# Inverse softmax sums by one small product and a way over DRAM, and K loaded for four heads at once, in a banded attention and mixture-of-experts kernel

## Chip, cores and metric

The kernel runs on one core of a Trainium2 chip. The metric is the device time of one execution in microseconds (us); the time of a kernel is the median of its runs.

## What is computed

Banded attention is followed by a mixture of experts. Attention has 4 batches, 8 heads, 768 positions and a head size of 64; each query sees the first 8 keys and the 96 keys up to itself, with a bias that grows with the distance.

```python
scores = scale * np.matmul(q, k.transpose(0, 1, 3, 2))
scores = np.where(keep, scores + bias, -1000000000.0)
a = np.exp(scores - scores.max(-1, keepdims=True))
a = a / (np.sum(a, axis=-1, keepdims=True) + 1e-09)     # the sums of the title
x = np.matmul(a, v)            # rearranged to 3072 x 512
# P: softmax of x @ w_gate, then 8 Sinkhorn iterations over rows and columns
for e in range(8):
    out += P[:, e:e + 1] * (np.maximum(x @ w1[e], 0.0) @ w2[e])
```

## The kernel before

**Units of work.** `Banded.work` lists 32 pieces n = (batch, half of the sequence, pair of heads g). A piece covers three query tiles of 128 (UT = 3) of two heads. `unit(u)` treats the four pieces of one batch and half; there are eight units. A piece has three groups of score tiles, so a unit has twelve groups t, taken two at a time (CHUNK) in six steps. With two pieces per six groups, a couple of pieces n = 2m and n = 2m + 1 spans three steps: t = 6m, 6m + 2 and 6m + 4.

**One step.** `ahead` computes scores and softmax four groups ahead (AHEAD). `flush` multiplies the turned scores of the step before with V into `o_ps`, and when a piece is complete it multiplies `o_ps` by `inv` on VectorE (line 404), casts it to `x` on ScalarE (line 405) and subtracts on VectorE (line 406). Then `turn` transposes the scores of this step (`t_ps`) and ScalarE copies them to `pT`. Then `between` is called three times: it emits filler work, which is the gate and the first layers of the mixture of experts for the unit before, and the sums `op` on GpSimd with their transfers to DRAM (`op_m`, from the pool `xout`). At the end of a step `prepare(n + 3)` transposes Q and K of a later piece and splits them into high and low parts (`qh`, `ql`, `kh`, `kl`), or, in the middle step of three, `invert` is called for both pieces. The filler lags by one unit and six slots, so the first unit has none.

**The inverse sums.** Exp leaves the sums of six columns (three tiles, two heads) on 128 query partitions. Line 316 adds EPS, line 317 inverts, and line 319 has ScalarE spread each column over 64 columns, to `inv` of 128 x 384. `invert` transposes its three tiles on TensorE into `r_ps`, and VectorE copies them back (line 414), so that each head's 64 partitions hold the row of inverse sums.

**PSUM.** `turned`, used by `prepare` and `invert`, takes a tile of tag "tp" from `self.ps`, which has two banks and serves `t_ps` also. In the first unit it takes the filler's banks, tag "fl", two as well.

**Loads.** All transfers are issued by SyncE, in one order. `load_qk(n)` loads Q of two heads with two transfers and K of two heads with five or seven, into `early_raw` for even n and `raw_qk` for odd n. It is called by `prepare(n - 2)`, once the buffer is free. `load_v(n)` loads V for four heads, thus for n and n + 1.

**Order.** TensorE's instructions keep the order of the program. On the other engines and on SyncE's queue a planner orders the instructions by its own reckoning of times. After attention come the dense layers by Strassen's scheme, to the end of the span; the change does not touch them.

Of the kernel before, what the change touches and what calls it, by code (L numbers as in the profile page):

```python
# [8 lines left out]
F32 = mybir.dt.float32  # L9
# [6 lines left out]
DRAM = bass.MemoryType.DRAM  # L16

P = 128
# [5 lines left out]
UT = 3  # L24
# [8 lines left out]
CHUNK = 2  # L33
# [81 lines left out]
class Banded:  # L115
# [5 lines left out]

    SLOTS = 8 * len(GROUPS)
    QK, V = UT + 4, 5
    RAW = QK * P + V * 2 * P
    BIAS1 = 4 * P

    SCRATCH = RAW + 3 * P

    def __init__(self, tc, q, k, v, early, n_bias):

        self.tc, self.nc = tc, tc.nc
        self.q, self.k, self.v = q, k, v
        self.H, self.D = q.shape[1], q.shape[3]
        assert n_bias == self.H * self.BIAS1
        self.bias1, rest = early, early[:, n_bias:]
        self.early_raw = rest[:, 0:self.RAW]
        self.d1 = early[:, n_bias - self.BIAS1:n_bias]
        self.d0 = rest[:, self.RAW:self.RAW + P]  # L140
        self.warm = rest[:, self.RAW + P:].bitcast(mybir.dt.bfloat16)
        self.work = [(b, half, g) for b in range(q.shape[0]) for half in range(2) for g in range(self.H // 2)]
        self.pending = []
        self.sums, self.inv, self.outs = {}, {}, {}
        self.pe = InOrder(tc)
        self.qk, self.vs, self.ready, self.scored = {}, {}, {}, {}

    def open(self, ctx, ident, idle):

        tc = self.tc  # L150
        self.ident, self.idle = ident, idle
        self.raw = ctx.enter_context(tc.tile_pool(name="f_raw", bufs=1, side="right"))
        self.bias0 = self.raw.tile([P, self.H, P], F32, name="bias0")
        self.opd = ctx.enter_context(tc.tile_pool(name="f_opd", bufs=2, side="right"))
        self.wrk = ctx.enter_context(tc.tile_pool(name="f_wrk", bufs=AHEAD + CHUNK, side="right"))
        self.ps = ctx.enter_context(tc.tile_pool(name="f_ps", bufs=2, space=PSUM))

    def distances(self, ng, nl):

# [57 lines left out]
            slot -= shift if slot > 1 + half else 0  # L217
            self.nc.sync.dma_start(out=dst[p:p + w, slot].rearrange("p (j d) -> p j d", j=heads), in_=src[row:row + w, tile])

    def load_qk(self, n):  # L220
        if n >= len(self.work):
            return
        b, half, g = self.work[n]
        if n % 2 == 0:
            t = self.early_raw[:, 0:self.QK * P]
        else:
            t = self.raw.tile([P, self.QK * P], F32, name="raw_qk")
        t = t.rearrange("p (t c) -> p t c", c=P)
        q_r, k_r = t[:, 0:UT], t[:, UT:]
        for j in range(2):  # L230
            src = self.q[b, 2 * g + j].rearrange("(t p) d -> p t d", p=P)
            self.nc.sync.dma_start(out=q_r[:, :, j * self.D:(j + 1) * self.D], in_=src[:, half * UT:(half + 1) * UT])
        self.load_heads(k_r, self.k, n, 2, [x for x in PIECES[half] if x[0] != 2 + half], 1)
        self.qk[n] = q_r, k_r

    def load_v(self, n):

        if n >= len(self.work):
            return
        if n % 4 == 0:  # L240
            t = self.early_raw[:, self.QK * P:]
        else:
            t = self.raw.tile([P, self.V * 2 * P], F32, name="raw_v")
# [8 lines left out]
    def prepare(self, n):  # L252

        if n >= len(self.work):
            return
        nc = self.nc
        self.ready[n] = tuple(self.opd.tile([P, w], F32R, name=name)
                              for name, w in (("qh", UT * P), ("ql", UT * P), ("kh", 4 * P + P // 2), ("kl", 4 * P + P // 2)))
        q_r, k_r = self.qk[n]
        qh, ql, kh, kl = self.ready[n]  # L260
        for src, hi, lo, nb in ((q_r, qh, ql, UT), (k_r, kh, kl, UT + self.work[n][1])):
            tp = self.turned("tp")
            for t in range(nb):
                self.pe.transpose(out=tp[:, t], in_=src[:, t], identity=self.ident)
            tp = tp.rearrange("p t c -> p (t c)")[:, 0:nb * P]
            nc.scalar.copy(out=hi[:, 0:nb * P], in_=tp)
            nc.vector.tensor_tensor(out=lo[:, 0:nb * P], in0=tp, in1=hi[:, 0:nb * P], op=ALU.subtract)
        self.load_qk(n + 2)

    def scores(self, ts):  # L270

# [21 lines left out]
    def softmax(self, t, s_list):  # L293


        nc, D = self.nc, self.D
        n, group = divmod(t, len(GROUPS))
        _, half, g = self.work[n]
        p_sb = self.wrk.tile([P, 2, 2, P], F32, name="p_sb")
        mx = self.wrk.tile([P, 2], F32, name="mx", bufs=4)  # L300
        if group == 0:
            self.sums[n] = self.wrk.tile([P, UT, 2], F32, name="sm", bufs=4)
        sm = self.sums[n]
        views = []
        for u, (j, i) in enumerate(GROUPS[group]):
            h = 2 * g + j
            pv = p_sb[:, u, 0:len(KEYS[half][i])]
            views.append(pv)
            nc.vector.tensor_tensor_reduce(out=pv, in0=s_list[u], in1=self.bias(h, half, i), scale=-(D ** -0.5), scalar=3.0e38,
                                           op0=ALU.add, op1=ALU.min, accum_out=mx[:, u:u + 1])  # L310
        for u, pv in enumerate(views):
            j, i = GROUPS[group][u]
            nc.scalar.activation(out=pv, in_=pv, func=AF.Exp, bias=mx[:, u:u + 1], scale=-1.0,  # L313
                                 accum_out=sm[:, i, j:j + 1])
        if group == len(GROUPS) - 1:
            nc.scalar.add(sm, sm, EPS)
            nc.vector.reciprocal(out=sm, in_=sm)
            self.inv[n] = self.wrk.tile([P, UT, P], F32, name="inv", bufs=3)
            nc.scalar.copy(out=self.inv[n].rearrange("p t (j d) -> p (t j) d", j=2),
                           in_=sm.rearrange("p t j -> p (t j)").unsqueeze(2).broadcast_to([P, 2 * UT, D]))  # L320
        return p_sb

    def blocks(self, n, group):
# [29 lines left out]
    def unit(self, u, xh, xl, between):  # L353

        NG, per = len(GROUPS), len(GROUPS) * (self.H // 2)
        if u == 0:
            self.load_qk(1)
            self.prepare(0)  # L360
            self.scale_bias(0)
            self.keep_warm(self.ps, "o", WARM0)
            self.ahead(range(0, CHUNK))
            self.load_v(2)
            self.prepare(1)
            for g in range(1, self.H // 2):
                self.scale_bias(g)
            for t in range(CHUNK, AHEAD, CHUNK):
                self.ahead(range(t, t + CHUNK))
            self.prepare(2)  # L370
        for t in range(u * per, (u + 1) * per, CHUNK):
            self.ahead(range(t + AHEAD, t + AHEAD + CHUNK))
            self.flush()
            for t1 in range(t, t + CHUNK):
                n, group = divmod(t1, NG)
                if group == 0:
                    self.outs[n] = self.ps.tile([P, UT, P], F32, name="o_ps", tag="o", bufs=2)
                g = n % (self.H // 2)
                self.pending.append((n, group, self.turn(t1), self.outs[n], xh[g], xl[g]))
            for c in (CHUNK, 1, 1):  # L380
                between(c)
            n = t // NG
            if t % (2 * NG) == CHUNK:
                self.invert(n)
                self.invert(n + 1)
            else:
                self.prepare(n + NG)
        self.idle = None

# [18 lines left out]
    def invert(self, n):  # L408
# [12 lines left out]

# [352 lines left out]
def pipeline(tc, attention, ident, moe, acc, scratch):  # L774
# [4 lines left out]
    nc = tc.nc  # L779
# [7 lines left out]
    with ExitStack() as top:  # L787
# [17 lines left out]
        NG = len(groups)  # L805
        xs = []
        for u in range(NU):
            c = u * UT % RT
# [188 lines left out]
        for n, (g, b) in enumerate(steps):  # L997
            p = g // NG
# [19 lines left out]
def kernel(  # L1018
# [12 lines left out]
    nc = tc.nc  # L1031
# [59 lines left out]
```

## Time and profile before

| | |
|---|---|
| median of 3 runs (lowest to highest) | 2199.67 us (2198.71 to 2199.75) |
| the profiled execution: time / span | 2199.65 us / 2197.9 us |
| busy share of the span: TensorE, VectorE, ScalarE, GpSimd | 99%, 60%, 34%, 51% |
| mean granted TensorE clock | 0.996 of 2.4 GHz |

The span runs from the first to the last instruction. Busy times of TensorE overlap, since its matmuls are pipelined; the pitch of a series is read from the start of one series to the start of the next.

### The profile page before, as it was taken

How to read it: one execution, taken by the hardware profiler on the slowest of the kernel's cores; microseconds unless marked ns; L12 is line 12 of the kernel's file. 1: busy time of each engine (PE TensorE's matmuls, PEld its weight loads, DVE VectorE, ACT ScalarE, POOL GpSimd, SP SyncE). 2: the span in 40 equal slices, each digit the busy share in tenths (PEclk: the TensorE clock that was granted, in tenths of full speed). 3: DMA queues.
4: the chain of work that ended last, by engine and by line, in shares of the span. 5: the costliest groups of instructions: out<-in, count | busy, mean ns of one | idle time of the engine just before them, and what ended most of it. 6: DMA issues, size and time to landing. Idle time of an engine off the chain costs nothing.

```text
span 2197.9 us, 29372 instructions
## 1 busy us (share of the span) xinstructions
PE 2177.2 (99%) x10851; PEld 1811.4 (82%) x10851; DVE 1329.1 (60%) x2348; ACT 757.1 (34%) x1540; POOL 1127.9 (51%) x1061
## 2 busy tenths in 40 slices
PE   7999999999999999999999999999999999999998
PEld 5888888888888888888888888888888888888887
DVE  6555546756656666665665665665566566566565
ACT  6677763322222222223232222222232223222231
POOL 5767565445445445445455554544454545545440
PEclk8999999999999999999999999999999999999999
DMA  5666553111111111171111111111611111111111
GB/s 122 162 194 175 144 165 128 48 58 48 49 58 48 55 51 48 58 259 50 57 48 58 48 49 58 49 51 55 201 57 49 49 58 49 58 48 49 58 39 50
DMA packets 207817, 173.47 MB, mean 79 GB/s; under 512 B 102704, under 2 KB 170800, under 8 KB 207664
## 3 DMA queue, kind: packets, MB, share of 16 engines
q1 hardware_dynamic: 207664, 171.51, 25.3%
q8 instruction: 87, 1.43, 0.3%
q14 instruction: 66, 0.54, 0.1%
HBM read 142.36 MB, written 29.10 MB: 78 GB/s over the span
## 4 chain that ended last, share of the span: by engine, by line
PE 97%; ACT 1%; DVE 1%; DMA 0%; SPq 0%; issue 0%; POOL 0%; ACTq 0%; DVEq 0%
PE y_ps L109 46%; PE bank_a L109 11%; PE bank_d L109 11%; PE bank_c L109 11%; PE bank_b L109 5%; PE h_ps L109 3%; PE o_ps L109 2%; PE s_ps L109 2%; PE t_ps L112 2%; PE tp L112 1%; PE r_ps L112 1%; PE g_ps L109 0%; ACT p_sb L313 0%; PE y_ps L705 0%; PE y_ps L704 0%; PE y_ps L703 0%
## 5 line engine op out<-in xcount | busy, mean ns | idle before, releaser
L990 DVE SCALAR_TENSOR_TENSOR early<-y_ps,pm,early 128x512 f32<-128x512 f32 x672 | 503.0, 749 | 241.8 <-PE y_ps L109 241.3
L563 POOL TENSOR_TENSOR wl<-wsum,wh 128x1280 fp32r<-128x1280 f32 x90 | 266.2, 2957 | 577.8 <-ACT wh L562 577.8
L585 POOL TENSOR_TENSOR wsum<-w1f 128x256 f32<-128x256 f32 x450 | 317.5, 740 | 319.1 <-DMA w1f<-in_moe_w_dram 319.1
L109 PE MATMUL y_ps<-w2h,h_set 128*128 128x512 f32 x1408 | 433.5, 389 | 0.0
L109 PE MATMUL y_ps<-w2h,x 128*128 128x512 f32 x1408 | 433.4, 389 | 0.0
L562 ACT CAST w2h<-w2f 128x1024 fp32r<-128x1024 f32 x90 | 94.8, 1054 | 688.6 <-issue 610.6
L109 PEld LDWEIGHTS y_ps<-w2h,h_set 128*128 128x128 f32 x1408 | 264.3, 188 | 54.9
L109 PEld LDWEIGHTS y_ps<-w2h,x 128*128 128x128 f32 x1408 | 264.3, 188 | 54.9
L109 PE MATMUL y_ps<-w2l,h_set 128*128 128x512 f32 x704 | 274.1, 389 | 0.1
L109 PE MATMUL y_ps<-w2l,x 128*128 128x512 f32 x704 | 273.9, 389 | 0.0
L109 PE MATMUL bank_a<-m,wh 128*128 128x512 f32 x696 | 242.8, 389 | 1.0 <-DVE h_set L635 1.0
L109 PE MATMUL bank_d<-x,wh 128*128 128x512 f32 x696 | 242.7, 389 | 0.0
L109 PE MATMUL bank_c<-x,wh 128*128 128x512 f32 x696 | 242.5, 389 | 0.0
L563 POOL TENSOR_TENSOR w2l<-w2f,w2h 128x1024 fp32r<-128x1024 f32 x90 | 216.0, 2400 | 48.5 <-ACT w2h L562 48.5
L675 DVE TENSOR_TENSOR early<-early,bank_d 128x512 f32<-128x512 f32 x90 | 62.0, 689 | 175.8 <-PE bank_d L109 171.8
L109 PEld LDWEIGHTS y_ps<-w2l,h_set 128*128 128x128 f32 x704 | 132.1, 188 | 27.8 <-DVE early L990 0.5
L109 PEld LDWEIGHTS y_ps<-w2l,x 128*128 128x128 f32 x704 | 132.1, 188 | 27.5
L109 PEld LDWEIGHTS bank_a<-m,wh 128*128 128x128 f32 x696 | 130.6, 188 | 29.0 <-DVE h_set L635 1.9
L109 PEld LDWEIGHTS bank_c<-x,wh 128*128 128x128 f32 x696 | 130.6, 188 | 27.1
L109 PEld LDWEIGHTS bank_d<-x,wh 128*128 128x128 f32 x696 | 130.6, 188 | 27.1
L109 PE MATMUL bank_a<-m,wl 128*128 128x512 f32 x348 | 135.4, 389 | 0.0
L109 PE MATMUL bank_d<-x,wl 128*128 128x512 f32 x348 | 135.4, 389 | 0.0
(233 smaller groups left out, 3480.8 us busy)
## 6 DMA issues: line engine op xcount, KB each, us to landing
w1f<-in_moe_w_dram SPq DMA_DIRECT2D x92, 512.0 KB, 3.5
w2f<-in_moe_w_dram SPq DMA_DIRECT2D x92, 512.0 KB, 3.4
x<-op_m SPq DMA_DIRECT2D x16, 512.0 KB, 7.6
op_m<-op SPq DMA_DIRECT2D x30, 256.0 KB, 2.8
m<-op_m SPq DMA_DIRECT2D x12, 512.0 KB, 7.2
out_dram<-early SPq DMA_DIRECT2D x24, 256.0 KB, 4.0
ys<-y_sb SPq DMA_DIRECT2D x21, 256.0 KB, 2.8
early<-ys SPq DMA_DIRECT2D x21, 256.0 KB, 4.1
```

What stands on the lines that cost most here:

```text
L109: return self.tc.keep_in_program_order(self.engine.matmul(*args, **kw))
L112: return self.tc.keep_in_program_order(self.engine.transpose(*args, **kw))
L562: self.nc.scalar.copy(out=hi, in_=full)
L563: self.nc.gpsimd.tensor_tensor(out=lo, in0=full, in1=hi, op=ALU.subtract)
L585: nc.gpsimd.tensor_tensor(out=s[:, n], in0=x, in1=y, op=op)
L675: tt(out=t3, in0=t3, in1=d, op=ALU.subtract)
L990: nc.vector.scalar_tensor_tensor(out=a, in0=y_ps, scalar=moe.pm[:, tt, e:e + 1], in1=a, op0=ALU.mult, op1=ALU.add)
```

## The change

For each piece `turn_sums` transposes the six columns of inverse sums directly, with one product, to six rows of 128. ScalarE copies the rows to SBUF, and SyncE stores them in DRAM (3 KB). `load_sums` reads them back with two transfers, each of which repeats three rows on the 64 partitions of one head; that is `inv`. The broadcast copy on ScalarE, the three transposes and VectorE's copy go. The products stand at other places: that of n = 2m at the end of the step t = 6m, ahead of `prepare`; that of n = 2m + 1 at the end of t = 6m + 2. `load_sums` of each stands one step after, behind the first `between`.

K is loaded for four heads at once, with five or seven transfers for two pieces, into `early_k` or `raw_k`, and `prepare` of an odd n calls for K of n + 3. Q is still loaded for each piece. `early` grows by 256 columns, the warm-up operand shares the place of a bias, and the pool `xout` has two buffers in place of three.

```diff
@@ Banded @@
+        self.dram = ctx.enter_context(tc.tile_pool(name="f_inv", bufs=4, space=DRAM))
-    def load_qk(self, n):
+    def load_q(self, n):
...
-        self.load_heads(k_r, self.k, n, 2, [x for x in PIECES[half] if x[0] != 2 + half], 1)
+    def load_k(self, n):
...
+        t = self.early_k if n % 4 == 0 else self.raw.tile([P, self.K], F32, name="raw_k")
+        t = t.rearrange("p (t c) -> p t c", c=2 * P)
+        self.load_heads(t, self.k, n, 4, [x for x in PIECES[half] if x[0] != 2 + half], 1)
+        self.ks[n], self.ks[n + 1] = t[:, :, 0:P], t[:, :, P:]
@@ prepare @@
-        self.load_qk(n + 2)
+        self.load_q(n + 2)
+        if n % 2:
+            self.load_k(n + 3)
@@ softmax @@
-            self.inv[n] = self.wrk.tile([P, UT, P], F32, name="inv", bufs=3)
-            nc.scalar.copy(out=self.inv[n].rearrange("p t (j d) -> p (t j) d", j=2),
-                           in_=sm.rearrange("p t j -> p (t j)").unsqueeze(2).broadcast_to([P, 2 * UT, D]))
@@ unit @@
-            self.load_qk(1)
+            self.load_q(1)
+            self.load_k(2)
...
-            for c in (CHUNK, 1, 1):
-                between(c)
             n = t // NG
-            if t % (2 * NG) == CHUNK:
-                self.invert(n)
-                self.invert(n + 1)
-            else:
+            between(CHUNK)
+            if t % (2 * NG):
+                self.load_sums(n)
+            between(1)
+            between(1)
+            if t % (2 * NG) == 0:
+                self.turn_sums(n)
+            elif t % (2 * NG) == CHUNK:
+                self.turn_sums(n + 1)
+            if t % (2 * NG) != CHUNK:
                 self.prepare(n + NG)
@@ invert @@
-        inv = self.inv[n]
-        r_ps = self.turned("r_ps")
-        for i in range(UT):
-            self.pe.transpose(out=r_ps[:, i], in_=inv[:, i], identity=self.ident)
-        self.nc.vector.tensor_copy(inv, r_ps[:, 0:UT])
+    def turn_sums(self, n):
+        tp = self.turned("r_ps")
+        self.pe.transpose(out=tp[0:2 * UT, 0], in_=self.sums.pop(n).rearrange("p t j -> p (t j)"), identity=self.ident)
+        rows = self.wrk.tile([2 * UT, P], F32, name="rows", bufs=2)
+        self.nc.scalar.copy(out=rows, in_=tp[0:2 * UT, 0])
+        self.spread[n] = self.dram.tile([2 * UT, P], F32, name="rows_d")
+        self.nc.sync.dma_start(out=self.spread[n], in_=rows)
+
+    def load_sums(self, n):
+        self.inv[n] = self.wrk.tile([P, UT, P], F32, name="inv", bufs=3)
+        src = self.spread.pop(n).rearrange("(t j) p -> j t p", j=2)
+        for j in range(2):
+            rows = slice(j * self.D, (j + 1) * self.D)
+            self.nc.sync.dma_start(out=self.inv[n][rows], in_=src[j].partition_broadcast(self.D))
@@ pipeline @@
-        xout = att.enter_context(tc.tile_pool(name="xout", bufs=3))
+        xout = att.enter_context(tc.tile_pool(name="xout", bufs=2))
@@ kernel @@
-    band.load_qk(0)
+    band.load_q(0)
+    band.load_k(0)
```

## Rows read from the trace of the kernel before

**Rows 1.** The page, first part: busy time, share of the span, instructions.
```profile
PE 2177.2 (99%) x10851; PEld 1811.4 (82%) x10851; DVE 1329.1 (60%) x2348; ACT 757.1 (34%) x1540; POOL 1127.9 (51%) x1061
```

**Rows 2.** Busy time by stretch: stretch, its length, engines; clock, DMA share, GB/s.
```profile
20.00:30.00 10.00, 7.95 (x53) 6.17 (x50) 5.52 (x23) 7.36 (x28) 4.58 (x6) 0.67 0.47 105
...
90.00:100.00 10.00, 8.87 (x66) 7.34 (x64) 2.96 (x13) 6.47 (x20) 9.43 (x11) 1.00 0.59 163
...
sum 280.00, PE 278.87 PEld 244.16 DVE 144.23 ACT 189.43 POOL 188.55; mean PE 19.92 PEld 17.44 DVE 10.30 ACT 13.53 POOL 13.47
```

**Rows 3.** Timeline of TensorE, 128 to 142 us: start, length, instruction, count.
```profile
131.87 1.15 PE L112 MATMUL tp<-ident,raw_qk 128*128 128x128 f32 x7
...
134.89 1.09 PE L112 MATMUL t_ps<-ident,p_sb 128*128 128x128 f32 x8
135.74 0.47 PE L109 MATMUL y_ps<-w2l,hh 128*128 128x512 f32 x1
...
139.14 0.82 PE L112 MATMUL r_ps<-ident,inv 128*128 128x128 f32 x6
...
140.79 1.09 PE L109 MATMUL o_ps<-pT,early 128*64 128x128 f32 x16
141.82 0.44 PE L112 MATMUL t_ps<-ident,p_sb 128*128 128x128 f32 x2
```

**Rows 4.** The tile r_ps: durations least/median/most in ns; idle time before it.
```profile
L112 PE MATMUL r_ps<-ident,inv x96: 270/272/421, 30.3 to 316.3; 128*128 128x128 f32 x96
L414 DVE COPY inv<-r_ps x32: 546/557/559, 31.2 to 316.8; 128x384 f32<-128x384 f32 x32
...
  PE r_ps L112: 30.0, 17
```

**Rows 5.** ScalarE around two turns, with the second turn; copies of few columns.
```profile
131.38 0.59 ACT L862 COPY y_sb<-y_ps 128x512 f32<-128x512 f32 x1
...
132.40 0.48 ACT L266 CAST qh<-tp 128x384 fp32r<-128x384 f32 x1 [0.33 <-PE tp L112]
...
191.65 0.93 PE L112 MATMUL tp<-ident,raw_qk 128*128 128x128 f32 x7
...
191.85 0.49 ACT L634 ACTIVATE hh<-h_ps 128x384 fp32r<-128x384 f32 x1 [0.49 <-PE h_ps L109]
...
L316 ACT ACTIVATE sm<-sm x32: 207/212/233, 21.1 to 309.0; 128x6 f32<-128x6 f32 x32
...
38.53 0.34 ACT L336 COPY pT<-t_ps 128x256 f32<-128x256 f32 x1
```

**Rows 6.** TensorE's waits to 345 us (total, times, longest); K near 91 us.
```profile
PEld tp L112 <- DMA raw_qk<-in_k_dram: 2.7, 5, 1.4
...
90.31 0.60 SPq L218 DMA_DIRECT2D raw_qk<-in_k_dram  x1
...
91.36 0.71 PE L112 MATMUL tp<-ident,raw_qk 128*128 128x128 f32 x5
```

**Rows 7.** Timeline of the start, SyncE's queue and TensorE.
```profile
16.67 3.46 SPq L218 DMA_DIRECT2D raw_v<-in_v_dram  x7
...
20.23 0.98 SPq L232 DMA_DIRECT2D raw_qk<-in_q_dram  x2
...
25.07 0.92 PE L112 MATMUL tp<-ident,raw_qk 128*128 128x128 f32 x2 [0.38 <-DMA raw_qk<-in_k_dram]
```

**Rows 8.** Timeline near 142 us; transfers (median us to landing); SyncE's longest wait.
```profile
141.91 2.56 SPq L232 DMA_DIRECT2D raw_qk<-in_q_dram  x2
142.27 0.56 DVE L404 TENSOR_TENSOR o_ps<-o_ps,inv 128x384 f32<-128x384 f32 x1
...
raw_qk<-in_q_dram SPq DMA_DIRECT2D x32, 96.0 KB, 2.8
...
early<-in_k_dram SPq DMA_DIRECT2D x40, 16.0 KB, 2.0
...
SPq L817 <- POOL op L611: 19.2, 9, 3.4
```

More of the change, by code (lines that the diff above doesn't have):

```diff
@@ L124 @@
     SLOTS = 8 * len(GROUPS)
-    QK, V = UT + 4, 5
-    RAW = QK * P + V * 2 * P
+    Q, K, V = UT * P, 4 * 2 * P, 5 * 2 * P
     BIAS1 = 4 * P
-    SCRATCH = RAW + 3 * P
+    SCRATCH = Q + K + V + P
     def __init__(self, tc, q, k, v, early, n_bias):
@@ L137, in __init__ @@
         self.bias1, rest = early, early[:, n_bias:]
-        self.early_raw = rest[:, 0:self.RAW]
+        self.early_q = rest[:, 0:self.Q]
+        self.early_k = rest[:, self.Q:self.Q + self.K]
+        self.early_v = rest[:, self.Q + self.K:self.Q + self.K + self.V]
+        self.d0 = rest[:, self.Q + self.K + self.V:]
         self.d1 = early[:, n_bias - self.BIAS1:n_bias]
-        self.d0 = rest[:, self.RAW:self.RAW + P]
-        self.warm = rest[:, self.RAW + P:].bitcast(mybir.dt.bfloat16)
+        warm = n_bias - 2 * self.BIAS1
+        self.warm = early[:, warm:warm + 2 * P].bitcast(mybir.dt.bfloat16)
         self.work = [(b, half, g) for b in range(q.shape[0]) for half in range(2) for g in range(self.H // 2)]
         self.pending = []
-        self.sums, self.inv, self.outs = {}, {}, {}
+        self.sums, self.spread, self.inv, self.outs = {}, {}, {}, {}
         self.pe = InOrder(tc)
-        self.qk, self.vs, self.ready, self.scored = {}, {}, {}, {}
+        self.qs, self.ks, self.vs, self.ready, self.scored = {}, {}, {}, {}, {}
     def open(self, ctx, ident, idle):
@@ L223, in load_qk @@
         b, half, g = self.work[n]
-        if n % 2 == 0:
-            t = self.early_raw[:, 0:self.QK * P]
-        else:
-            t = self.raw.tile([P, self.QK * P], F32, name="raw_qk")
+        t = self.early_q if n % 2 == 0 else self.raw.tile([P, self.Q], F32, name="raw_q")
         t = t.rearrange("p (t c) -> p t c", c=P)
-        q_r, k_r = t[:, 0:UT], t[:, UT:]
         for j in range(2):
             src = self.q[b, 2 * g + j].rearrange("(t p) d -> p t d", p=P)
-            self.nc.sync.dma_start(out=q_r[:, :, j * self.D:(j + 1) * self.D], in_=src[:, half * UT:(half + 1) * UT])
-        self.load_heads(k_r, self.k, n, 2, [x for x in PIECES[half] if x[0] != 2 + half], 1)
-        self.qk[n] = q_r, k_r
+            self.nc.sync.dma_start(out=t[:, :, j * self.D:(j + 1) * self.D], in_=src[:, half * UT:(half + 1) * UT])
+        self.qs[n] = t
+    def load_k(self, n):
+        if n >= len(self.work):
+            return
+        half = self.work[n][1]
+        t = self.early_k if n % 4 == 0 else self.raw.tile([P, self.K], F32, name="raw_k")
+        t = t.rearrange("p (t c) -> p t c", c=2 * P)
+        self.load_heads(t, self.k, n, 4, [x for x in PIECES[half] if x[0] != 2 + half], 1)
+        self.ks[n], self.ks[n + 1] = t[:, :, 0:P], t[:, :, P:]
     def load_v(self, n):
@@ L239, in load_v @@
             return
[L240 to L243, printed above, removed]
+        t = self.early_v if n % 4 == 0 else self.raw.tile([P, self.V], F32, name="raw_v")
         t = t.rearrange("p (t c) -> p t c", c=2 * P)
@@ L258, in prepare @@
                               for name, w in (("qh", UT * P), ("ql", UT * P), ("kh", 4 * P + P // 2), ("kl", 4 * P + P // 2)))
-        q_r, k_r = self.qk[n]
+        q_r, k_r = self.qs[n], self.ks[n]
         qh, ql, kh, kl = self.ready[n]
@@ L379, in unit @@
                 self.pending.append((n, group, self.turn(t1), self.outs[n], xh[g], xl[g]))
-            for c in (CHUNK, 1, 1):
-                between(c)
             n = t // NG
-            if t % (2 * NG) == CHUNK:
-                self.invert(n)
-                self.invert(n + 1)
-            else:
+            between(CHUNK)
[8 more added lines that the diff above has]
+            if t % (2 * NG) != CHUNK:
                 self.prepare(n + NG)
@@ L406, in flush @@
         self.nc.vector.tensor_tensor(out=xl, in0=o_ps, in1=xh, op=ALU.subtract)
-    def invert(self, n):
-        inv = self.inv[n]
-        r_ps = self.turned("r_ps")
-        for i in range(UT):
-            self.pe.transpose(out=r_ps[:, i], in_=inv[:, i], identity=self.ident)
-        self.nc.vector.tensor_copy(inv, r_ps[:, 0:UT])
+    def turn_sums(self, n):
[11 more added lines that the diff above has]
+            self.nc.sync.dma_start(out=self.inv[n][rows], in_=src[j].partition_broadcast(self.D))
 class Dense:
```

## The prediction

> **What bounds the kernel now.** I read the page first: TensorE is busy for 99% of the span [rows 1], so only what shortens or stretches TensorE's own sequence can move the time. Then I read the busy time of the engines in stretches, because the change touches the attention stage alone. From 60 to 340 us TensorE lacks 1.13 us of work, and all of it lies in 90 to 100 us; before that it runs with holes, and between 20 and 30 us the granted clock is 0.67, a mean of the two levels 1.2 and 2.4 GHz [rows 2]. So the attention stage has two parts: the first unit (to about 60 us), which is held up by loads, ScalarE and VectorE, and seven units in which TensorE never stops. In the second part a VectorE or ScalarE instruction that goes away is worth nothing by itself; a TensorE instruction that goes away is worth its pitch, and a new wait of TensorE costs all of its length. Then the timeline of TensorE for the pitches, that of ScalarE around the turns of Q and K, and that of SyncE's queue for the transfers.
>
> **The products that go.** Today each head pair n has three transposes of `inv` (96 in all) [rows 4], done for two n at once at the end of the second step of each six. Eight transposes of scores take from 134.89 to 135.74, which is 0.106 us each [rows 3]; six are 0.64 us. Afterwards there is one product for each n: the stationary operand has six columns, the moving one is the identity of 128. The trace has none such. Its price lies between that of a full transpose, 0.106, and that of the value products, which load 64 columns and move 128: 16 of them take from 140.79 to 141.82, 0.064 us each [rows 3]. The six-column load is nearer to the latter, so I take 0.064. Two n then cost 0.13 in place of 0.64, a saving of 0.51 us; with 0.106 it would be 0.43. There are 16 such couples: 15 at full clock are 7.7 us (6.4 with the dearer price), and the first one, turned at half clock, counts double: 1.0. Together 8.7 us off TensorE. The Trainium skill (TensorE: Matmul & The Clock Gate, section LDWEIGHTS) has the load's time grow with the columns loaded and not with the rows, 128 columns at 107 ns; the pitches of 0.106 and 0.064 agree with that for 128 and 64 columns. By it the six-column load would vanish behind the 128 moving columns, which the page puts near 0.056 us, and the sum would be 0.3 us better.
>
> **A new wait that they bring.** The products stand elsewhere now: that for n=2m at the end of the first step of six, straight ahead of `prepare`. `turned` and the score transposes share the two banks of tag "tp". The order there becomes: score transposes into banks A and B, filler work, `r_ps` into A, Q's turn into B, K's turn into A again. K's turn must wait until ScalarE has copied `rows` out of A, and between lie only three transposes, 0.32 us. Before, Q and K took A and B, whose copies were long done. The path: a product takes 0.27 us from its start to its result [rows 4]; ScalarE followed by 0.04 us (turn of raw_qk at 131.87, third transpose at 132.08, ended at 132.35, cast at 132.40) [rows 3, 5]; the copy of 6 rows of 128 is not in the trace, and lies between the 0.21 us of 6 elements and the 0.34 of 256 [rows 5], so I take 0.28. Bank A is free at 0.27 + 0.04 + 0.28 = 0.59, and I add 0.05 for the signal back; TensorE is there at 0.064 + 0.32 = 0.38. The wait is 0.26 us if ScalarE is free. In the case at 131.87 the copy y_sb that began at 131.38 would be over; in the case at 191.65 the ReLU `hh` begins at 191.85 and holds ScalarE until 192.34, 0.38 us beyond the moment at which the product's result stands [rows 5]. Of the eleven turns of an odd n after the first unit five have a ReLU beginning like this, six look like the first case. So 0.26 + 0.5 x 0.38 = 0.45 us, 14 times after the first unit: 6.3 us given back. Bounds: 14 x 0.1 = 1.4, if the copy is fast and the ReLU comes later, and 14 x 0.95 = 13.3, if the ReLU is ahead each time and another half microsecond of ScalarE with it.
>
> **The copies that go.** ScalarE's broadcast copy `inv` and VectorE's copy back (32 times 0.557 us, and 30.0 us in which VectorE stood waiting for `r_ps`) [rows 4] are not on TensorE's path from 60 us on: 0. In the first unit they are part of the chain; I count them with it.
>
> **K for four heads.** A K transfer for a couple of n replaces two; each n had five or seven, so 16 x 6 = 96 issues on SyncE go. `turn_sums` adds one and `load_sums` two for each n: 96 come. At 0.49 us each (two Q loads took 0.98) [rows 7] SyncE's total is unchanged. What moves is when: K of an odd n is there with the even one, and the next load follows three turns ahead and not two. TensorE's waits for K were 2.7 us in five, the longest 1.4 [rows 6]. That one is the hole of 90 to 100 us: the last piece of K was issued at 90.31, while the turn of that K began at 91.36 [rows 6]. It goes: 1.1 us by the stretches [rows 2]. In the first unit, the V transfer at 16.67 and Q at 20.23 stood behind five K issues that no longer come there: Q of n=3 is issued 5 x 0.49 = 2.5 us earlier, and its K is already in; the turn that ended with the DMA wait at 25.07 to 25.99 [rows 7] can be over some 2 us earlier. I take 2.0 (0 to 3.5, the upper with a share of the copies). The first K load doubles in bytes, but it is behind the mask arithmetic of VectorE, so 0.
>
> **The way over DRAM.** Product, copy, store, two loads, multiply. From the turn at 131.87 to the multiply by `inv` at 142.27 there are 10.4 us [rows 3, 8]. The trip takes 0.6 for product and copy, 0.49 for the issue, 2.0 to 2.8 to land, two issues 0.98 and 2.8 to land [rows 7, 8]: 6.9 to 7.7. So 3 us are left for standing in SyncE's queue, on two occasions. I take 0 for the forecast; the rest is a rival. **`xout` with two buffers**: GpSimd's second sum waits for the transfer two earlier; SyncE already waited 19.2 us for `op` in nine cases [rows 8]. GpSimd is no bound of the stage, so I put 0.5 us (0 to 4, if Q's loads queue behind it).
>
> **The sum.** The profiled execution took 2199.65 us, 1.75 above its span, and equals the median of 2199.67. 2199.65 - 8.7 + 6.3 - 1.1 - 2.0 + 0.5 = 2194.65. What a measurement of this kernel can tell from no change is about 0.2%, 4.4 us; the forecast is only just beyond.
>
> **The rivals.** *The shared bank takes it all*: the wait for `rows` costs 0.7 us or more, because the planner puts ReLU and other copies ahead of it: 14 x 0.7 = 9.8, and the start-up gives only 1. 2199.65 - 8.7 + 9.8 - 1.1 - 1 + 0.5 = 2199.2: no change. For it speaks that ScalarE is in order and half the turns meet a ReLU; against it that the broadcast copy that often stood there is gone.
>
> *The way over DRAM is late.* SyncE's queue is in order and often behind: Q's next load, freed by the turn at 131.87, went out at 141.91, 10 us later [rows 3, 8]. If both the store and the loads stand like this, the trip is over 20 us and the multiply waits. It heads VectorE's queue; behind it stand the splits, the next scores' masks and, through ScalarE's cast of x, the copies of the turned scores, which TensorE needs within one step. It decides when the two queue times exceed the 3 us by more than VectorE's reserve, somewhere between 0 and a step of 7 us. At half a microsecond of TensorE for each of the 28 later n, it is 14 us: 2194.65 + 14 = 2208.7, slower. Against it: the planner places the multiply where its own reckoning has the loads land, and the ends of the multiply are needed by no TensorE work soon. The Trainium skill (DMA: Bandwidth & Descriptors, section Latency and other measured facts) has HBM's latency rise from 0.2 us on average to 2 us under load; that would lengthen each of the two landings, and no row here separates it.
>
> *The wait is hidden and the first unit gives more*: ScalarE, freed of the copy, takes `rows` at once and the denser start raises the clock earlier. 2199.65 - 8.7 + 1.4 - 1.1 - 3.5 = 2187.8.
>
> **Chances and range.** Forecast 0.55, with a range of its own from 2190 to 2198; nearly three quarters of it lie below 2195.3, which is 0.2% under the median. Shared bank 0.15; late DRAM way 0.18; hidden wait 0.12. Faster: 0.40 + 0.12 = 0.52. Same: 0.15 + 0.15 + 0.01 = 0.31. Slower: 0.17. The range goes from 2188.5 to 2204: below lies half of the hidden wait, above most of the late way.
>
> **What would show it.** Right: 32 `r_ps` products in place of 96, at a pitch under 0.11; no wait for in_k at 90 us; an idle time of TensorE before K's turn of some 0.3 to 0.6 us, put down to `rows`, once in six steps; a first unit that ends 2 to 4 us earlier; from 340 us on a shift and nothing else. Wrong: idle time of VectorE at the multiply put down to the load of `inv`, with TensorE waiting behind it; waits for in_q; or K's turn following Q's without a hole.

## The result, and the profile after

The changed kernel takes 2213.62 us (median of 6 runs, 2212.80 to 2218.03) against 2199.49 (2198.71 to 2199.81) for the kernel before, run beside it. The ratio is 1.0070, with a 95% interval of 1.0057 to 1.0083. It is 14 us slower; the forecast was 2194.65 with a range up to 2204, so the time lies outside. The profiled execution took 2213.48 us with a span of 2211.5, 13.6 more than the span before.

The page of the changed kernel, its first part:

```profile
PE 2179.1 (99%) x10787; PEld 1804.5 (82%) x10787; DVE 1314.3 (59%) x2316; ACT 752.7 (34%) x1540; POOL 1127.4 (51%) x1061
```

Beside [rows 1], TensorE has 64 instructions fewer, as the change intends, and VectorE 32. These sums and shares tell nothing of the 14 us. The waits do.

Waits of all engines in the changed kernel to 360 us (what was waited for, us in total, times, longest):

```profile
DVE o_ps L416 <- DMA inv<-rows_d: 44.9, 16, 6.9
...
ACT x L417 <- DVE o_ps L416: 30.4, 13, 6.0
...
PE o_ps L109 <- DVE pT L342: 7.8, 2, 4.9
...
PEld tp L112 <- ACT rows L425: 6.3, 13, 1.7
...
PE tp L112 <- ACT pT L342: 4.3, 5, 1.2
```

and the longest of SyncE's queue in the same stretch:

```profile
SPq L436 <- DMA rows_d<-rows: 19.4, 17, 3.1
```

Half of the 32 multiplies by `inv` wait for the load of `inv`, 2.8 us each in the mean. ScalarE's cast of `x` waits behind the multiply, and TensorE behind the copies `pT` of VectorE or ScalarE: 7.8 and 4.3 us. (Not all of these copies are ScalarE's: 6 of the 96 are VectorE's, all in the first unit.) SyncE too stands 19.4 us, for the store of `rows` to land before it may issue the loads. No turn of K waits for `in_k` any more ([rows 6] had 2.7 us).

Busy time by stretch in the changed kernel (columns as in [rows 2]):

```profile
34.00:36.00 2.00, 0.00 (x0) 0.00 (x0) 0.00 (x0) 0.00 (x0) 2.00 (x2) 1.00 0.47 128
...
38.00:40.00 2.00, 2.00 (x13) 1.67 (x14) 2.00 (x10) 1.47 (x5) 0.00 (x0) 0.50 0.57 127
...
52.00:54.00 2.00, 0.23 (x4) 0.23 (x6) 1.44 (x4) 0.84 (x2) 0.00 (x0) 1.00 0.41 136
...
56.00:58.00 2.00, 1.70 (x8) 0.88 (x7) 1.16 (x4) 2.00 (x8) 0.00 (x0) 0.50 0.88 225
...
60.00:340.00 280.00, 271.24 (x2246) 229.74 (x2244) 130.18 (x485) 186.17 (x582) 176.40 (x206) 1.00 0.61 171
...
335.00:340.00 5.00, 2.32 (x11) 1.57 (x9) 1.12 (x2) 3.48 (x6) 1.76 (x1) 1.00 0.76 198
340.00:345.00 5.00, 4.74 (x14) 3.80 (x15) 1.38 (x2) 2.31 (x6) 4.86 (x4) 0.66 0.97 340
```

From 60 to 340 us TensorE now lacks 8.76 us of work where it lacked 1.13 [rows 2]. Behind three holes the granted clock fell to its lower level, 1.2 GHz: it is 0.50 from 38 to 42 us, where TensorE had not been busy at all from 34 to 36; 0.50 from 56 to 60, where it had been busy for 0.23 of the 2 us from 52; and 0.66, a mean of the two levels, from 340 to 345, where it had been busy for less than half of 335 to 340. So a hole costs its length and something behind it.

**Where the time went.** TensorE keeps the order of the program, so the 48 steps of attention can be laid beside each other: for each step I took the start of its score transposes (`t_ps`) in the timeline of TensorE, and subtracted the same in the kernel before. Negative is earlier. Six steps are a unit, and units are counted from 1 here (the code and the expectations count from 0). E1 to E10 are the experiments below; each line is one profiled execution.

| us against the kernel before | step 3 | 9 | 12 | 24 | 33 | 42 | 48 | end of span |
|---|---|---|---|---|---|---|---|---|
| the change | -4.0 | +5.6 | +7.3 | +6.3 | +6.0 | +9.7 | +8.9 | +13.6 |
| E1, K for four heads alone | -3.7 | -4.5 | -4.5 | -6.1 | -6.1 | -6.1 | -6.1 | -6.4 |
| E3, multiply without the wait | -4.0 | -4.2 | -4.1 | +2.6 | +2.0 | +1.9 | +1.6 | +13.7 |
| E4, store by ScalarE, loads by GpSimd | -3.1 | +4.8 | +6.0 | +4.1 | +3.5 | +4.2 | +3.5 | +3.7 |
| E6, store by ScalarE | -1.4 | +5.7 | +6.9 | +4.8 | +4.5 | +5.2 | +6.4 | +7.3 |
| E7, trip in units 2 to 7 | -3.7 | -4.6 | +1.6 | -0.5 | +0.4 | +2.3 | +3.3 | +3.0 |
| E9, trip in units 3 to 7 | -4.0 | -4.8 | -4.8 | -7.2 | -2.5 | +1.6 | +4.6 | +4.4 |
| E10, E9 with the store by ScalarE | -4.0 | -4.8 | -4.8 | -7.0 | -6.8 | -7.7 | -5.5 | -4.1 |

The first line is the whole story of the change: it is 4.0 us ahead by step 3, loses 11.3 us in steps 3 to 12, gains 1.3 in the twenty steps that follow (1.6 in E1), loses 3.7 in steps 33 to 42, gets 0.8 back, and loses 4.7 behind the last step. The lines are single executions, and that of E9 is the slowest of its eleven, 2204.05 us against a median of 2200.69.

**The first trip.** Timeline of the changed kernel from 24 to 38 us (start, length, queue or engine, instruction; in brackets the idle time before it and what ended it):

```profile
24.20 0.24 ACT L425 COPY rows<-r_ps 6x128 f32<-6x128 f32 x1
...
25.78 1.70 SPq L233 DMA_DIRECT2D raw_q<-in_q_dram  x2
...
27.58 0.38 SPq L427 DMA_DIRECT2D rows_d<-rows  x1
...
28.05 4.80 SPq L223 DMA_DIRECT2D raw_k<-in_k_dram  x7
...
32.92 1.33 SPq L436 DMA_DIRECT2D inv<-rows_d  x2
...
36.63 0.56 DVE L416 TENSOR_TENSOR o_ps<-o_ps,inv 128x384 f32<-128x384 f32 x1 [6.91 <-DMA inv<-rows_d]
37.10 0.68 DVE L342 COPY pT<-t_ps 128x512 f32<-128x512 f32 x1
37.28 0.48 ACT L417 CAST x<-o_ps 128x384 fp32r<-128x384 f32 x1 [5.96 <-DVE o_ps L416]
...
37.84 1.12 PE L109 MATMUL o_ps<-pT,early 128*64 128x128 f32 x8 [4.88 <-DVE pT L342]
```

The rows are ready at 24.44. The store goes out at 27.58, 3.1 us later, behind loads of V, weights and Q. Seven K issues (4.80 us) are next in the queue, so the loads go out at 32.92, and the multiply runs at 36.63: 12.4 us from the start of the copy (14.5 from the product at 22.15, for ScalarE came to its copy late), against the 6.9 to 7.7 that the prediction reckoned for the trip from the product on. The multiply heads VectorE's queue, which stands for 6.91 us; the copy `pT` behind it is what TensorE wants at 37.84. TensorE stood for 4.88 us.

**The last trip.** The same view of the changed kernel behind its last product of sums, which starts at 325.22:

```profile
325.53 0.25 ACT L425 COPY rows<-r_ps 6x128 f32<-6x128 f32 x1 [1.01 <-PE r_ps L112]
326.09 2.09 SPq L839 DMA_DIRECT2D x<-op_m  x4
328.23 0.36 SPq L427 DMA_DIRECT2D rows_d<-rows  x1
...
331.81 1.52 SPq L436 DMA_DIRECT2D inv<-rows_d  x2
...
335.92 0.57 DVE L416 TENSOR_TENSOR o_ps<-o_ps,inv 128x384 f32<-128x384 f32 x1 [5.99 <-DMA inv<-rows_d]
...
340.26 4.61 PE L641 MATMUL x_ps<-x,plus_minus 128*128 128x512 f32 x12 [1.99 <-ACT y_sb L884]
```

Here nothing follows that could cover it: 10.4 us from copy to multiply, and behind it products at a granted clock of 0.66.

### The profile page after: what moved, and what is told of

Same layout as the page of the kernel before. It is cut to its first block, busy times and chain, and to the rows that moved or that the text cites. A ratio compares the mean times of both kernels' runs of the same rounds, so it can differ in the third digit from the quotient of the medians.

```text
span 2211.5 us, 29231 instructions
## 1 busy us (share of the span) xinstructions
PE 2179.1 (99%) x10787; PEld 1804.5 (82%) x10787; DVE 1314.3 (59%) x2316; ACT 752.7 (34%) x1540; POOL 1127.4 (51%) x1061
## 4 chain that ended last, share of the span: by engine, by line
PE 95%; DMA 2%; ACT 1%; DVE 1%; SPq 1%; issue 1%; POOL 0%; DVEq 0%; ACTq 0%
PE y_ps L109 45%; PE bank_a L109 11%; PE bank_d L109 11%; PE bank_c L109 11%; PE bank_b L109 5%; PE h_ps L109 2%; PE t_ps L112 2%; PE o_ps L109 2%; PE s_ps L109 2%; PE tp L112 1%; DMA inv<-rows_d 1%; ACT p_sb L322 0%; PE g_ps L109 0%; PE y_ps L727 0%; PE y_ps L726 0%
## 5 line engine op out<-in xcount | busy, mean ns | idle before, releaser
L109 PE MATMUL bank_c<-x,wl 128*128 128x512 f32 x348 | 135.4, 389 | 0.0
```

The source lines that it names most:

```text
L109: return self.tc.keep_in_program_order(self.engine.matmul(*args, **kw))
```

## The experiments

Eleven kernels, with the kernel before run beside each. Diffs are against the changed kernel unless said otherwise. Times are medians; the ratio is to the kernel before as run beside it, with its 95% interval.

**E1: K for four heads alone.** The old inverse comes back (broadcast copy, three transposes, copy back); K for four heads and two `xout` buffers stay.

```diff
+            self.inv[n] = self.wrk.tile([P, UT, P], F32, name="inv", bufs=3)
+            nc.scalar.copy(out=self.inv[n].rearrange("p t (j d) -> p (t j) d", j=2),
+                           in_=sm.rearrange("p t j -> p (t j)").unsqueeze(2).broadcast_to([P, 2 * UT, D]))
...
-            between(CHUNK)
-            if t % (2 * NG):
-                self.load_sums(n)
-            between(1)
-            between(1)
+            for c in (CHUNK, 1, 1):
+                between(c)
+            if t % (2 * NG) == CHUNK:
+                self.invert(n)
+                self.invert(n + 1)
```

> Only the K part of the change: K for four heads at once (and xout with two buffers); the inverse sums are spread, transposed and copied as before. Theory A (the way over DRAM is what costs: the multiply by inv waits for loads that stand in SyncE's queue, and holds VectorE, ScalarE and then TensorE): no trip, so only K's gain is left, 2194 to 2198 us. Theory B (the K transfers in one burst, or xout with two buffers, crowd SyncE's queue and that costs): 2205 to 2214 us. Theory C (the wait of K's turn for rows in the shared bank costs): as A here.

Measured: 2193.28 us (9 runs, 2192.74 to 2193.91), ratio 0.9974 [0.9964, 0.9984]; 5.4 us faster than the kernel before. In the table it gains 4.5 us by step 9 and 1.6 more by step 24. Busy time by stretch in E1:

```profile
60.00:340.00 280.00, 280.00 (x2299) 244.89 (x2298) 144.65 (x508) 187.24 (x570) 180.17 (x207) 1.00 0.58 167
90.00:100.00 10.00, 10.00 (x77) 8.99 (x76) 4.30 (x18) 6.91 (x24) 9.61 (x9) 1.00 0.62 188
```

TensorE lacks nothing from 60 to 340; the hole of 90 to 100 [rows 2] is closed. All the loss therefore belongs to the sums' part of the change (product, bank and trip): the change as a whole is 20 us slower than E1, 12 of them by step 12.

**E2: the sums' part alone**, on the kernel before: product, store and loads, K still for two heads, three `xout` buffers. Its diff is the change's, without `load_q` and `load_k`.

> Only the sums part: one product, store, two loads; K for two heads and xout with three buffers as before. 96 more issues on SyncE. Theory A: the trip is late as in the change and K's early gain is missing, 2210 to 2220 us. Theory B: 2195 to 2201 us. Theory C: 2205 to 2214 us, with the holes of TensorE before K's turn and not behind the multiply.

Measured: 2241.87 us (4 runs), 1.0197 [1.0180, 1.0214]. That is slower than any of the three theories said. The trip without K's savings costs 43 us, spread over all units; from 60 to 340 TensorE is busy for 253.16 us. The two parts of the change hang together: K for four heads saves as many issues as the trip spends (96), and it is worth 5.4 us alone, but 28 under the trip. That it is the number of issues, and not the earlier K, was not tested apart.

**E3: the multiply does not wait.** It takes a tile of ones; store and loads stay.

```diff
-        self.nc.vector.tensor_tensor(out=o_ps, in0=o_ps, in1=self.inv.pop(n), op=ALU.mult)
+        self.nc.vector.tensor_tensor(out=o_ps, in0=o_ps, in1=self.ones.unsqueeze(1).broadcast_to([P, UT, P]), op=ALU.mult)
+        self.inv.pop(n)
```

> The whole change with all its transfers, but the multiply takes a tile of ones in place of inv, so nothing waits for the loads (the output is not normalised by the sums). Theory A: the loss goes although the queue carries the same transfers, 2190 to 2196 us. Theory B: the burst and the queue are as before, 2205 to 2214 us. Theory C: 2205 to 2214 us, since the product, the bank and the copy rows are unchanged.

Measured: 2212.40 us (4 runs), 1.0059 [1.0042, 1.0075]. The total seems to clear the wait of blame, and must be read by steps. Up to step 14 E3 lies within 1.8 us of E1: with the same transfers on the same queue, the 12 us of the first two units are gone, so they were the multiply's wait. Then there are two losses of another kind, seen in its waits to 360 us:

```profile
ACT w2h L585 <- DMA inv<-rows_d: 12.5, 1, 12.5
...
PE g_ps L751 <- DVE x L419: 9.2, 1, 9.2
...
PE h_ps L109 <- ACT y_sb L886: 4.3, 2, 4.1
```

At step 15 it loses 5.8 us, with TensorE waiting 4.1 for ScalarE's `y_sb`, whose spill to DRAM goes through SyncE's queue; there the load stands until the store has landed (19.8 us in 16 waits in E3), and all that is queued behind it stands too. That this made the spill late is read from the timeline and not tested. The 12 us in the tail are of the experiment's own making: nobody reads `inv`, and the next owner of its place, a weight cast, is the first to wait for the load. So E3 shows the wait's part in the first two units, and cannot show the rest.

**E4: both transfers off SyncE's queue**, the store to ScalarE's, the loads to GpSimd's.

```diff
-        self.nc.sync.dma_start(out=self.spread[n], in_=rows)
+        self.nc.scalar.dma_start(out=self.spread[n], in_=rows)
...
-            self.nc.sync.dma_start(out=self.inv[n][rows], in_=src[j].partition_broadcast(self.D))
+            self.nc.gpsimd.dma_start(out=self.inv[n][rows], in_=src[j].partition_broadcast(self.D))
```

> The whole change, but the store is issued by ScalarE right behind its copy rows and the two loads by GpSimd, not by SyncE. Theory A: store and loads no longer stand behind K, V and Q, the trip takes some 5 us, 2191 to 2198 us. It is 2200 or more if GpSimd's long sums hold the loads as SyncE's queue did. Theory B: 2200 to 2208 us, for SyncE loses 96 issues. Theory C: 2208 to 2214 us.

Measured: 2202.71 us (10 runs), 1.0019 [1.0009, 1.0028], 11 us better than the change. (The time lies in the range of theory B too, but E1 had excluded that theory.) From step 12 on nothing is lost any more, in the tail either (+6.0 at step 12, +3.7 at the end). So the later losses of the change come from SyncE's queue. The first two units lose as before: on GpSimd's queue the loads stand behind casts and subtractions of weights. Timeline of E4, GpSimd and VectorE:

```profile
31.45 1.04 POOL L594 CAST w2h<-w2f 128x1024 fp32r<-128x1024 f32 x1 [0.36 <-DMA w2f<-in_moe_w_dram]
...
32.43 1.50 POOL L436 DMA_DIRECT2D inv<-rows_d  x2
33.93 2.36 POOL L595 TENSOR_TENSOR w1l<-w1f,w1h 128x1024 fp32r<-128x1024 f32 x1
36.23 2.36 POOL L595 TENSOR_TENSOR w2l<-w2f,w2h 128x1024 fp32r<-128x1024 f32 x1
36.84 0.57 DVE L416 TENSOR_TENSOR o_ps<-o_ps,inv 128x384 f32<-128x384 f32 x1 [5.85 <-DMA inv<-rows_d]
...
38.52 1.26 POOL L436 DMA_DIRECT2D inv<-rows_d  x2
```

The first pair of loads goes out as a cast of weights ends, though ScalarE had issued the store at 25.18; the second stands behind two weight subtractions of 2.36 us. Over the attention stage the multiply's waits for `inv` are 13.6 us in 4, where the change has 44.9 in 16.

**E5: the product in the middle of the step**, ahead of the two last pieces of filler, so that K's turn no longer finds the rows in its bank.

```diff
-            between(1)
-            between(1)
             if t % (2 * NG) == 0:
                 self.turn_sums(n)
             elif t % (2 * NG) == CHUNK:
                 self.turn_sums(n + 1)
+            between(1)
+            between(1)
```

> The whole change, but the product of the sums stands behind the first of the three calls of filler work, not at the end of the step: the copy rows has the rest of the filler to end in before K's turn needs the bank, and the trip begins some 2 us earlier. Theory C (shared bank, 0.45 us in each of 16 couples): TensorE's waits for rows go, 6 to 7 us less than the change, 2205 to 2208 us. Theory A alone (the trip stands in SyncE's queue): the trip's lateness shrinks by 2 us in the first unit and in the tail only, 2207 to 2212 us. Both: 2200 to 2206 us.

Measured: 2212.20 us (4 runs, 2209.69 to 2222.22), 1.0074 [1.0050, 1.0098]. The weight load's wait for `rows` falls from 6.3 us in 13 to 2.3 in one, and the time stays where it was within what these runs can tell: the interval reaches from 2209.7 to 2220.3 us, above what the theory of the shared bank asked. In the profiled execution, the fastest of the four, the multiply's waits for `inv` fall as well, to 29.6 us in 10, so these runs put no price on the bank by itself. They show that it is not the main cause.

**E6: only the store leaves SyncE's queue** (E4's first line alone).

> The whole change, but ScalarE issues the store right behind its copy, so the store no longer stands in SyncE's queue; the loads do. Theory A: one of the two queue times goes (3 us in the first unit), the multiply's waits fall by about a third, 2204 to 2210 us. If it is only the loads that are late: 2212 to 2215 us. Theory C: unchanged, 2213 us.

Measured: 2207.65 us (5 runs), 1.0039 [1.0025, 1.0053], 6 us better than the change. The multiply's waits for `inv` fall from 44.9 us in 16 to 20.1 in 8, and SyncE's standing for the stores from 19.4 us in 17 to 9.0 in 5. The first two units stay lost (+6.9 at step 12); there the K issues in front of the loads remain.

The Trainium skill (DMA: Bandwidth & Descriptors, section Issuing engines are not separate DMA queues) says that transfers of all issuing engines run on the same 16 DMA engines, and that issuing from another one saves only sequencer time, usually small beside the transfer. No run here shows the first apart. On the second, the issue of a store is short here too, 0.398 us in the median of 32; yet moving these 32 is worth 6 us, for with the issues go the stores' standing in SyncE's queue and part of SyncE's standing for them.

**E7: the trip in units 2 to 7 alone**; the first and the last unit have the old inverse.

```diff
+            old = u in (0, 7)
...
-                self.load_sums(n)
+                old or self.load_sums(n)
...
-            if t % (2 * NG) == 0:
+            if t % (2 * NG) == 0 and not old:
...
-            elif t % (2 * NG) == CHUNK:
+            elif t % (2 * NG) == CHUNK and not old:
                 self.turn_sums(n + 1)
+            if t % (2 * NG) == CHUNK and old:
+                self.invert(n)
+                self.invert(n + 1)
```

> The first and the last unit take the inverse sums as before (copy, three transposes, copy back), the six units between take the trip over DRAM by SyncE; K for four heads throughout. Theory A as the trace places it (loss in the first unit, where there is no filler, and behind the last step): those 11 + 5 us go, 2195 to 2199 us. If the loss follows the number of trips: 24 of 32 of it stay, 2207 to 2211 us.

Measured: 2202.15 us (10 runs), 1.0015 [1.0006, 1.0025]. It goes with E1 through step 9, and loses 6.0 us at step 10, at its first trip, where the multiply waits 5.7 us. The time lies between the two expectations. So the loss isn't tied to the first unit: it moved to where the trip begins. Only the loss behind the last step is gone.

**E8: E7 with the product in the middle of the step and the store by ScalarE** (the edits of E5 and E6).

> As the kernel with the trip in the six middle units, with the product behind the first call of filler and the store issued by ScalarE. If the product's saving of 0.5 us for a couple comes out once bank and queue are out of the way: 12 x 0.5 = 6 us below the kernel with K alone, 2186 to 2190 us. If the loads in SyncE's queue still hold the multiply in single places: 2191 to 2197 us.

Measured: 2200.12 us (10 runs), 1.0003 [0.9994, 1.0013]. That is above both expectations. It loses 7.3 us against E1 at step 9, in another way. Timeline of E8, SyncE's queue, ScalarE and TensorE:

```profile
48.58 6.73 SPq L223 DMA_DIRECT2D raw_v<-in_v_dram  x9
...
53.71 0.54 ACTq L442 DMA_DIRECT2D rows_d<-rows  x1
54.29 0.59 ACT L273 CAST kh<-tp 128x512 fp32r<-128x512 f32 x1 [4.48 <-DMA early<-in_q_dram]
...
55.65 0.66 PE L112 MATMUL t_ps<-ident,p_sb 128*128 128x128 f32 x4 [3.46 <-DVE kl L274]
```

ScalarE, with its rows copied at 48.97 and its cast `qh` over at 49.81, issues the store only at 53.71, and K's cast stands behind it. After that E8 gains on E1, 3.0 us from step 10 to step 42, which is 0.28 for each couple of pieces, net of the waits that E8 still has. Where there are none it gains more: it stands 7.40, 6.98, 6.55 and 6.12 us behind E1 at steps 13, 16, 19 and 22, which is 0.43 a couple.

**E9: the trip in units 3 to 7 alone**, product in the middle, all by SyncE (E7 with `old = u in (0, 1, 7)`, and E5). **E10** is E9 with the store by ScalarE.

> The trip over DRAM in units 2 to 6 only (20 of 32 pieces), by SyncE, with the product behind the first call of filler; units 0, 1 and 7 keep copy, three transposes and copy back; K for four heads throughout. If the loss sits where SyncE's queue is full of V and expert weights (first unit and the entry to the second) and behind the last step, nothing of it is left: 10 couples x 0.3 us (the fall seen in the trace of the middle units) below K alone, 2189 to 2192 us. If each trip costs by its place in SyncE's queue, wherever it stands: 2196 to 2201 us.

> As the run before it, with the store issued by ScalarE. If SyncE's standing still until the store has landed is what holds its queue in these units: 1 to 3 us less than the run before it. If not: within 1 us of it, or more where ScalarE stands behind its own issue.

Measured: E9 2200.69 us (11 runs, 2197.57 to 2204.05), 1.0006 [0.9997, 1.0015]; E10 2195.51 (11 runs), 0.9985 [0.9976, 0.9994]. E9 goes with E1 and ahead of it, up to step 24. At step 25 it loses 4.9 us, at step 37 another 4.3, both at the entry of a unit. Timeline of E9 there:

```profile
153.13 4.10 SPq L223 DMA_DIRECT2D early<-in_k_dram  x5
...
157.28 1.28 SPq L451 DMA_DIRECT2D inv<-rows_d  x2
...
158.66 0.44 SPq L442 DMA_DIRECT2D rows_d<-rows  x1
...
160.51 1.23 SPq L451 DMA_DIRECT2D inv<-rows_d  x2
160.90 0.57 DVE L423 TENSOR_TENSOR o_ps<-o_ps,inv 128x384 f32<-128x384 f32 x1 [5.53 <-DMA inv<-rows_d]
...
162.62 0.55 PE L112 MATMUL tp<-ident,raw_k 128*128 128x128 f32 x3 [3.34 <-ACT pT L346]
```

The pattern is that of the first trip: K issues, then the loads, the multiply late, TensorE standing for 3.34 us. With the store by ScalarE (E10) the first loss shrinks to 1.5 us and the second is gone; by the medians E10 is 5.2 us faster than E9, more than the 1 to 3 expected. At step 42 it stands 1.6 us ahead of E1, 0.3 of it from the start: up to there the trip pays, though little. Then it loses 2.2 us by step 45, where the last multiply of the trip waits 3.97 us for its load (283.63), and 1.7 more behind the last step, where no trip stands and which I can't explain. In all E10 ends 2.3 us of span behind E1.

**E11: two `xout` buffers alone**, on the kernel before.

```diff
-        xout = att.enter_context(tc.tile_pool(name="xout", bufs=3))
+        xout = att.enter_context(tc.tile_pool(name="xout", bufs=2))
```

> The kernel before with two buffers of xout in place of three and nothing else. The prediction put 0.5 us (0 to 4) on it: 2199 to 2200 us. Theory B (fewer buffers hold GpSimd, GpSimd's results hold SyncE): 2202 us or more.

Measured: 2199.23 us (10 runs), 1.0003 [0.9994, 1.0012]: nothing that can be measured. But in its profiled execution the hole of 90 to 100 is closed as in E1 (TensorE busy for 10.00 of it), and a wait of 0.6 us for K comes later. So how much of the 1.6 us that E1 gains there is K's, and how much the order that comes with two buffers, these runs don't separate.

## Why the prediction was wrong

The step that failed is the one under "The way over DRAM", which ends "So 3 us are left for standing in SyncE's queue, on two occasions. I take 0 for the forecast". In its place the runs showed a trip of 12.4 us at the start and 10.4 at the end, 44.9 us of waiting in 16 of the 32 multiplies, and TensorE standing behind them, up to 4.88 us at once; without that wait (E3) the 12 us of the first two units are gone. The rival of the same name came true, at a chance of 0.18.

- **The slack was read in the wrong place.** The 10.4 us between turn and multiply come from steps of the middle units, 6.7 us each, full of filler. In the first unit, where there is none, a step takes 3.7 to 4.8 us (steps 3 to 6 of the kernel before start at 33.57, 37.29, 41.53 and 46.37). The trip has hardly more than one step and a half there, by these starts an estimated 6 to 7 us: less than the prediction's own 6.9 to 7.7, without any queue.
- **Both issues stand in a queue in order.** The prediction saw a Q load go out 10 us late [rows 8], and took it for what a rival would need; it was what happened, with shorter times. In the first trip the store stood 3.1 us and the loads went out 5.3 after it; at two entries of units the loads stood behind K in the same way (E9, behind 153.13).
- **A wait that I did not list.** The loads may be issued only when the store has landed, and SyncE stands for that: 19.4 us in 17 waits, with everything behind it. The Trainium skill (DMA: Bandwidth & Descriptors, section Two DMAs through the same engine are not ordered) has the issuing engine wait for the first transfer's semaphore before it issues the dependent one; the trace agrees. By it the wait can't be dropped, only moved to a queue on which nothing urgent follows.
- **The rival's price was of the right order and wrong in shape.** It said 14 us at half a microsecond for each of 28 later pieces. The loss against E1 is 20 us: 12 by step 12, nothing to step 33, 3 to 4 in steps 33 to 42, and 5 behind the last step. VectorE's reserve, left open between 0 and a step, is about 2 us where there is filler: in the changed kernel, waits of the multiply of 3.0 to 3.2 us (at 230.57 and 252.59) cost TensorE 1.13 and 0.96, and those of 4.3 and 6.9 us (52.56 and 36.63) cost 2.93 and 4.88. "From 340 us on a shift and nothing else" fell too, for the last trip reaches past the last step.

What held:

- **K for four heads** was reckoned at 3.1 us less 0.5 for `xout`. E1 measured 5.4; the start was sized too small, 4.5 in place of 2.0. The hole at 91 us closed as forecast, though E11 closes it without K. E11 also confirms the 0.5 as next to nothing in the time.
- **The product.** The tile r_ps in the changed kernel (least/median/most ns):

```profile
L112 PEld LDWEIGHTS r_ps<-ident,sm x32: 83/84/130, 21.9 to 325.0; 128*6 128x6 f32 x32
L112 PE MATMUL r_ps<-ident,sm x32: 271/272/422, 22.1 to 325.2; 128*6 128x128 f32 x32
L425 ACT COPY rows<-r_ps x32: 237/254/256, 24.2 to 325.5; 6x128 f32<-6x128 f32 x32
```

  The 96 products became 32 of the same length as in [rows 4]. The copy takes 0.254 us where I took 0.28. The price of a product was sized too low. TensorE in E8:

```profile
92.69 0.39 PE L109 MATMUL y_ps<-w2h,hh 128*128 128x512 f32 x1
92.92 0.27 PE L112 MATMUL r_ps<-ident,sm 128*6 128x128 f32 x1
...
93.26 0.39 PE L109 MATMUL y_ps<-w2h,hl 128*128 128x512 f32 x1
```

  One other `y_ps` product starts in between, at 92.94; their own pitch is 0.23 us, so two take 0.46, and with the product among them they take 0.57. It costs 0.11 us, as much as a full transpose, and not 0.064: few columns to load did not make it cheaper. (The two pitches of the prediction agree only roughly with a load that grows with its columns, too: half of 0.106 is 0.053, not 0.064.) In the changed kernel, too, Q's turn starts 0.11 behind it (138.45 and 138.56). The dearer price in the prediction, 0.43 us for a couple, is what E8 gains where nothing waits. So the 8.7 us of the sum are by an estimate from these numbers some 7.3.
- **The shared bank.** Predicted 6.3 us in 14 waits after the first unit; the weight load's wait for `rows` is 6.3 us in 13, the first unit's among them. The balance of a middle couple, 0.51 less 0.45, was predicted at 0.06 us, next to nothing; against E1 the change loses 0.3 us from step 12 to step 33 and gains 0.3 from step 13, in seven couples. That is nothing either way, so the steady part of the forecast stood; the entries and the ends decided.
- **Two slips in the sums.** K's turn stands behind the product in 13 couples after the first unit, not 14 (the last couple has no piece left to prepare), which makes 5.9 us of the 6.3. And the sum of the third rival leaves out the 0.5 for `xout`; with it, it is 2188.3. Neither bears on the outcome.

**What stays open.** Why the planner's order puts the loads of `inv` behind K at some unit entries (steps 25 and 37) and not at others, I can't say; that the place of the loads in the queue decides is shown by E4, E6 and E10, but not why it is chosen. A trip with the loads ahead of K in the queue, or with the multiply a step later, was not tried. Of the 12 us lost to E1 by step 12, TensorE's two waits of 4.88 and 2.93 us are 7.8; how much of the rest is the lower clock behind them was not measured apart. The landing times under load, which the prediction cited beside the late trip, can't be told from the queue by these runs.

The best version is E1: K for four heads and the old inverse, 2193.28 us, 0.9974 [0.9964, 0.9984] of the kernel before.

## What to carry to other kernels

Before a value leaves the core's engines for a way over DRAM, lay the whole trip (copy, store's place in the issue queue, landing, load's place in the queue, landing) against the shortest stretch between producer and consumer, at the start, at entries and at the end, and not against a middle step. An engine instruction that waits for it at the head of an in-order queue passes its wait on, less the reserve of that engine. And two edits that share a resource, here SyncE's issues, have to be priced together: one of them was worth 5 us alone and 28 beside the other.

## What the runs showed of the hardware

- A store issued by ScalarE can stand for long: in E8 its issue came at 53.71, 3.9 us after ScalarE's last instruction, in the course of nine V issues of SyncE that take 6.73 us. The profile puts the end of ScalarE's idle time down to a load of Q, which neither the store nor the cast behind it reads. The issue itself is short, 0.26 us in the median of the 24 in E8. E6 has the same in its first unit, beside seven K issues of SyncE; there the issue came 2.9 us after the copy:

```profile
28.50 5.14 SPq L223 DMA_DIRECT2D raw_k<-in_k_dram  x7
30.24 0.25 ACT L425 COPY rows<-r_ps 6x128 f32<-6x128 f32 x1
33.39 0.27 ACTq L427 DMA_DIRECT2D rows_d<-rows  x1
33.70 0.51 ACT L322 ACTIVATE p_sb<-p_sb,mx 128x256 f32<-128x256 f32 x1 [3.21 <-DMA raw_k<-in_k_dram]
```

  So ScalarE's queue was no free way out while SyncE issued a burst. What holds the store was not tested.
- The issues are not equal. A load of `inv`, which repeats three rows on 64 partitions, takes SyncE 0.604 us in the median of 64 (0.573 to 1.397), a store of `rows` 0.398 (0.288 to 1.717); I had reckoned 0.49 for all. An issue of K takes 0.436 or 0.448 us in the median in the kernel before (`early`, `raw_qk`), so by an estimate from these medians the 96 issues that come cost SyncE 51 us and the 96 that go 42: its total is not unchanged.
- The weight load of six columns is recorded with 84 ns in the median against 140 for 128 columns, while the product's own record is the same 272 ns for both.
